# Four q buffers, three v buffers, a gate product over two blocks and one key per operation in a fused attention and gated FFN kernel

## The chip, the core and the metric

The kernel runs on one core of one Trainium2 chip. The metric is the device time of one execution in microseconds (us); lower is better. Engine names follow the profile: PE is TensorE (PEld its weight loads), DVE is VectorE, ACT is ScalarE, POOL is GpSimd and SP is SyncE. POOL issues the loads from HBM, SP the output stores and the DMA transposes.

## What is computed

Pooled attention feeds a feed-forward layer with a convolved gate. Cut to what matters:

```
B, H, S, D = 8, 8, 576, 64           # q, k, v: (B, H, S, D) float32
k_p, v_p = means over 8 neighbouring positions of k and v       # 72 of 576 rows stay
attn = softmax(q @ k_p^T / 8)
x = (attn @ v_p) with the heads side by side                    # (B, 576, 512)
h = max(x @ w_in, 0)                                            # (B, 576, 1024)
conv = sum over 3 taps of conv_w[tap] * h shifted by tap - 1    # along the sequence
out = (h * sigmoid(conv)) @ w_out                               # (B, 576, 512) float32
```

## The kernel before

The eight batches go in four groups of two (g0 to g3). A group has nine attention tiles of 128 rows: tiles 0 to 3 belong to its first batch, tile 4 is shared, 5 to 8 belong to the second.

- **Loads and preparation.** A batch's q, k and v come in by POOL queue, cast to bf16 in tiles of 128 partitions. q is transposed on PE in two halves (`prep_q`, L578) into PSUM and copied to `qT` by DVE or ACT (`copy_q`, L588). k is pooled by matmuls for b0 and b1 (`prep_k`) and, from group 1 on, for a whole group on DVE in three halving additions (`pool_pair`, L520), turned on PE (`turn_pair`, L526) and copied to `kT` (L539). v is pooled on DVE in three additions (L548) and masked into `vm` (L552). Rings hold 2 buffers of q (`qp`), 2 of v and 1 of k (`kk`).
- **Attention of a tile.** Scores on PE (L630, or L617 in quarter form), the row maximum on DVE (`negm`, L643), its subtraction on PE (group 0, L663) or DVE (`sd`, L655), exp on ACT (`e`, L681), the transposition of `e` on PE with a copy (groups 0 and 1: L692, L706) or as a DMA from SP (groups 2 and 3: L701), the values on PE (L717), reciprocal and division on DVE (`x`, L730, L732), and the transposition of `x` into `xT`, again on PE with a copy or as a DMA (L741).
- **FFN of a batch.** First layer on PE (`ffn_in`, L762; for b0 by tiles, `ffn_in_tile`, L783), relu on ACT (L771, L793) into `hT`. The convolution is matmuls with diagonal matrices in quarters of the PE array (`ffn_conv`, L844), two 128-wide blocks of d_ff at a time. ACT takes tanh of half of it into `tg` (L855). `ffn_gate` adds 1 on DVE (L872 for even blocks, L867 twice for odd ones, where the halves are swapped) and multiplies by `hT` into `gT` (L873), once per block: 8 products a batch. The second layer (`ffn_out`, L878) takes 36 tiles of 8 matmuls; ACT or DVE copies each tile out (L889) and SP stores it (L901).

Each engine executes its instructions in the order of its program; an instruction that waits holds up those behind it. That order is made by the class `Graph`: each piece of work is an `Op` with a key, with estimates of time on each engine, and with the buffers (`Token`) that it uses. `Graph.order` places them one after another: whichever can start next and has the lowest key goes first, and a copy that DVE or ACT may do goes where it can start. In the kernel before, keys come from a few numbers per class (`ATT`, `OUT`, `PREP_V` and others, and `NUDGE` per class and batch). The estimates only set the order: on the chip, semaphores release the instructions.

The waits of POOL's queue matter too: at most eight loads are under way, and a load whose buffer is in use waits for it, with everything behind it.

Of the kernel before, what the change touches and what calls it, by code (L numbers as in the profile page):

```python
# [33 lines left out]
class Graph:  # L34
# [8 lines left out]
    STAY = 2454.96  # L43
    LAZY = 7.6
    BLOCK, PRELUDE, FETCH, FETCH_LOADING = 256, 66, 3.4, 6.2
    BEAT, PHASE, HALVE, RAISE = 3.413, 0.7, 0.56, 0.85
    BESIDE_LOADS = 3.5
    SPARES = 150
    IN_FLIGHT = 8
    ATT = -1061.14  # L50
    SPREAD = -6040.17
    PREP_K = -4446.75
    KPOOL = -172.25
    KTURN = 242.29
    PREP_Q = 12175.88
    PREP_V = 17420.36
    GATE = 249.38
    CONV = -19287.15
    QCONV = -11687.66
    OUT = 13057.35  # L60
    LAST = 18152.59
    FIRST = 19180.99
    V0 = -19763.16
    DW = 22027.64
# [4 lines left out]
    URGENT = -28942.38  # L69
    NUDGE = {  # L70
# [203 lines left out]
def kernel(  # L274
# [826 lines left out]
    def prepared(g, t):  # L1101
# [3 lines left out]
        return need  # L1105

    def add_att(g, t, key):
        key += nudge("a", groups[g][t >= 5])
        rows = rows_of(g, t)
        b0 = groups[g][0]  # L1110
        split = len(parts(g, t)) == 2
# [158 lines left out]
```

## Time and profile before

| what | before |
|---|---|
| median of 3 runs (lowest, highest) | 248.94 us (248.41, 249.13) |
| profiled execution, its own time | 248.62 us |
| its span, first to last instruction | 246.9 us |
| PE, DVE, ACT busy | 218.5, 175.9, 149.1 us |
| mean granted PE clock | 0.975 of full speed |
| loaded and stored by DMA | 31.51 MB |

Of the 248.62 us of the profiled execution, 246.9 lie between its first and last instruction and 1.72 around them; its own time is 0.32 below the median of the three runs. Busy times of PE and PEld overlap, and a matmul's row includes its latency: four matmuls of 512 columns that follow each other have rows of 0.38 each and take 0.86 together. How far PE is from its work is therefore read from the idle time between its rows.

### The profile page before, as it was taken

Reading aid. Unit: us, or ns where it says so; the run is one execution under the profiler, and the core shown is the slowest. Engines: PE = TensorE matmul, PEld = TensorE weight load, DVE = VectorE, ACT = ScalarE, POOL = GpSimd, SP = SyncE. Lnnn points to the kernel's source line nnn. Section 1 sums busy time; section 2 is a strip of 40 time slices with the busy share of each in tenths; the row PEclk is TensorE's granted clock in tenths of the full one; section 3 lists DMA queues with packets and bytes.
Section 4 is the critical chain, followed back from the end, with each engine's and each line's share of the span. In section 5 each row is a group of like instructions: output and inputs, shape, how many; then the busy total and the mean of one; then the engine's idle time right before and its main releaser. Section 6 shows DMA issues by size and latency. Waiting matters only on the chain.

```text
span 246.9 us, 7525 instructions
## 1 busy us (share of the span) xinstructions
PE 218.5 (89%) x3206; PEld 149.4 (61%) x3206; DVE 175.9 (71%) x397; ACT 149.1 (60%) x245; POOL 27.9 (11%) x45
## 2 busy tenths in 40 slices
PE   7187999899699999968999992999999899999992
PEld 2174898776566566746764651776764477676440
DVE  7278757999999989789999992466689701965200
ACT  2046568688797666658676731575784456766531
POOL 7931303010320012200000100000000000000000
PEclk9779999999999999999999998899999999999998
DMA  6999999990799749913744799388125965600475
GB/s 92 176 203 207 208 206 208 205 191 5 105 185 240 168 75 210 206 24 61 93 88 93 145 136 130 70 142 144 22 48 125 127 127 120 128 4 3 92 165 127
DMA packets 44006, 31.51 MB, mean 128 GB/s; under 512 B 23596, under 2 KB 39364, under 8 KB 43972
## 3 DMA queue, kind: packets, MB, share of 16 engines
q0 software_dynamic: 16288, 16.26, 41.4%
q1 hardware_dynamic: 27604, 14.64, 32.2%
q8 instruction: 25, 0.41, 0.7%
q14 instruction: 9, 0.07, 0.2%
q10 hardware_dynamic: 80, 0.13, 0.1%
HBM read 32.52 MB, written 9.44 MB: 170 GB/s over the span
## 4 chain that ended last, share of the span: by engine, by line
PE 39%; DVE 32%; DMA 16%; ACT 5%; issue 5%; POOL 2%; DVEq 0%; ACTq 0%; POOLq 0%
PE psum L878 11%; PE psum L762 11%; DVE gT L873 6%; DMA eT<-e 6%; DVE negm L643 5%; PE psum L844 5%; DVE gT L867 4%; DMA qp<-in_q_dram 4%; DMA v<-in_v_dram 4%; DVE sd L655 4%; DVE x L732 3%; PE psum L783 3%; PE psum L717 3%; DVE v L548 3%; ACT tg L855 2%
## 5 line engine op out<-in xcount | busy, mean ns | idle before, releaser
L878 PE MATMUL psum<-w_out_sb,gT 128*128 128x512 bf16 x288 | 69.6, 379 | 0.3 <-ACT tg L855 0.2
L762 PE MATMUL psum<-xT,w_in_sb 128*128 128x288 bf16 x448 | 62.8, 290 | 0.7 <-ACT tg L855 0.6
L762 PEld LDWEIGHTS <-w_in_sb 128*128 128x128 bf16 x448 | 42.1, 99 | 14.5 <-issue 0.8
L771 ACT ACTIVATE hT<-psum 128x576 bf16<-128x576 f32 x56 | 35.3, 650 | 23.8 <-PE psum L762 23.6
L855 ACT ACTIVATE tg<-psum 128x576 bf16<-128x576 f32 x64 | 37.9, 649 | 12.3 <-PE psum L844 8.9
L878 PEld LDWEIGHTS <-gT 128*128 128x128 bf16 x288 | 26.1, 98 | 24.9 <-issue 0.4
L844 PE MATMUL psum<-hT,dw 64*64 64x288 bf16 (+4 forms) x1152 | 30.2, 246 | 0.0
L844 PEld LDWEIGHTS <-dw 64*64 64x64 bf16 x1152 | 24.3, 107 | 9.7 <-issue 9.1
L889 ACT COPY osb<-psum 128x512 f32<-128x512 f32 (+1 forms) x34 | 19.7, 580 | 16.6 <-PE psum L878 14.2
L643 DVE TENSOR_REDUCE negm<-psum 128x8 f32<-128x576 f32 (+1 forms) x36 | 26.4, 749 | 2.5 <-PE psum L630 1.9
L732 DVE TENSOR_TENSOR x<-psum,r 128x512 bf16<-128x512 f32 x36 | 24.9, 691 | 1.2
L681 ACT ACTIVATE e<-sd 128x576 bf16<-128x576 f32 x27 | 18.2, 682 | 10.0 <-DVE sd L655 9.2
L717 PE MATMUL psum<-vm,eT 128*128 128x130 bf16 (+5 forms) x240 | 18.4, 224 | 6.3 <-DMA eT<-e 5.5
L730 DVE RECIPROCAL r<-psum 128x8 f32<-128x8 f32 x36 | 7.2, 201 | 22.1 <-PE psum L717 22.0
L717 PEld LDWEIGHTS <-eT 128*128 128x128 bf16 (+1 forms) x240 | 14.5, 101 | 11.6 <-DMA eT<-e 6.6
L867 DVE TENSOR_SCALAR gT<-tg 64x576 bf16<-64x576 bf16 x64 | 20.0, 313 | 1.2
L655 DVE TENSOR_TENSOR sd<-psum,negm 128x576 f32<-128x576 f32 x27 | 19.8, 749 | 0.3
L872 DVE TENSOR_SCALAR tg<-tg 128x576 bf16<-128x576 bf16 x32 | 9.8, 306 | 10.8 <-ACT tg L855 10.8
L630 PE MATMUL psum<-kT,qT 128*128 128x144 bf16 (+1 forms) x136 | 12.8, 226 | 3.8 <-DVE kT L539 1.3
L873 DVE TENSOR_TENSOR gT<-tg,hT 128x576 bf16<-128x576 bf16 x32 | 14.7, 458 | 1.1
L873 DVE TENSOR_TENSOR gT<-gT,hT 128x576 bf16<-128x576 bf16 x32 | 14.6, 458 | 1.1
L630 PEld LDWEIGHTS <-qT 128*128 128x128 bf16 (+1 forms) x136 | 9.3, 98 | 7.8 <-issue 5.1
(74 smaller groups left out, 206.5 us busy)
## 6 DMA issues: line engine op xcount, KB each, us to landing
out_dram<-osb SPq DMA_DIRECT2D x71, 128.0 KB, 2.4
v<-in_v_dram POOLq DMA_DIRECT2D x8, 512.0 KB, 12.0
qp<-in_q_dram POOLq DMA_DIRECT2D x7, 576.0 KB, 12.5
kk<-in_k_dram POOLq DMA_DIRECT2D x3, 1152.0 KB, 10.9
w_in_sb<-in_moe_w_in_dram POOLq DMA_DIRECT2D x2, 512.0 KB, 12.7
w_out_sb<-in_moe_w_out_dram POOLq DMA_DIRECT2D x1, 1024.0 KB, 18.7
kk<-in_k_dram POOLq DMA_DIRECT2D x2, 288.0 KB, 7.2
kk<-in_k_dram POOLq DMA_DIRECT2D x1, 576.0 KB, 14.2
```

The costliest lines, as they stand in the source:

```text
L630: nc.tensor.matmul(out=heads[lo:hi, f], lhsT=buf("qT", b)[:, f, a, t % 5 * P:t % 5 * P + hi - lo], rhs=buf("kT", b)[:, 2 * f + a, :], star ...
L643: nc.vector.tensor_reduce(out=a["m"][0:rows], in_=a["s"][0:rows, :, 0:2 * KW].rearrange("p a (h s) -> p a h s", s=Sp), axis=AX.X, op=OP.ma ...
L655: nc.vector.tensor_tensor(out=a["d"][0:rows], in0=a["s"][0:rows, :, 0:2 * KW].rearrange("p a (h s) -> p a h s", s=Sp), in1=a["m"][0:rows]. ...
L717: nc.tensor.matmul(out=a["o"][lo:hi, h // 4, (h % 4) * (D + 1):(h % 4 + x1 - x0) * (D + 1)], lhsT=a["eT"][:, j, lo:hi], rhs=buf("vm", b)[: ...
L732: nc.vector.tensor_tensor(out=a["x"][0:rows].rearrange("p (a h d) -> p a h d", a=2, d=D), in0=ov[:, :, :, 0:D], in1=r[0:rows].unsqueeze(3) ...
L762: nc.tensor.matmul(out=banks(ps)[:, j, 0:SC], lhsT=w_in_block(dc, fb), rhs=buf("xT", g)[:, dc, i * S + j * SC:i * S + (j + 1) * SC], start ...
L771: nc.scalar.activation(out=buf("hT", b)[:, fb, :].rearrange("p (a s) -> p a s", a=2), in_=banks(ps)[:, :, 0:SC], func=ACT.Relu, scale=0.5,)
L844: nc.tensor.matmul(out=banks(pss[r ^ c])[c * D:(c + 1) * D, j, lo:hi], lhsT=dw[r * D:(r + 1) * D, tap * n_fb + fb, :], rhs=hT[r * D:(r + 1 ...
L855: nc.scalar.activation(out=tg.rearrange("p (a s) -> p a s", a=2), in_=banks(ps)[:, :, 0:SC], func=ACT.Tanh, scale=0.5,)
L867: nc.vector.tensor_scalar(out=gate[r * D:(r + 1) * D], in0=tg[(1 - r) * D:(2 - r) * D], scalar1=1.0, scalar2=None, op0=OP.add)
L873: nc.vector.tensor_tensor(out=gate, in0=tg, in1=buf("hT", b)[:, fb, :], op=OP.mult)
L878: nc.tensor.matmul(out=bank(ps)[0:rows, :], lhsT=buf("gT", g)[:, fb, t * P:t * P + rows], rhs=w_out_sb[:, fb, :], start=(fb == 0), stop=(f ...
```

## The change

Four edits. The rings of q and v get 4 and 3 buffers (from 2 and 2). The gate adds 1 for an even block into `gT` in place of `tg`, and one product over two blocks, 128 x 2 x 576, takes the place of two over 128 x 576. Every operation gets a key of its own from a table `KEYS`, in the order in which the operations were added, which overrides the class keys; some of the planner's estimates are changed as well. The rest of the diff gives the operations further names for nudges.

```diff
     PIPE = {"PE": 0.24, "DVE": 0.14, "ACT": 0.14, "POOL": 0.10, "SP": 0.0}
...
-    STAY = 2454.96
-    LAZY = 7.6
+    STAY = 0.1228
+    LAZY = 0.4188
...
-    BESIDE_LOADS = 3.5
+    BESIDE_LOADS, HOLD = 4.5, 0.3
...
+    GAP = 0.0
+    KEYS = (
+        -1000.0, 2.454, -4.193, 1.702, -1000.0, -1000.0, 2.8993, 1.9366, 7.1326, -1.4149, 7.4, 7.98,
...
+    )
...
     def order(self):
+        for o, key in zip(self.ops, self.KEYS):
+            o.key = key
...
-                if any(e2 == e and key2 < self.URGENT and key2 < o.key and s2 < s + d - 0.1 for s2, e2, _, key2 in later):
+                if any(e2 == e and key2 + self.GAP < o.key and s2 < s + d - 0.1 for s2, e2, _, key2 in later):
...
                     o.end = s + d + fixed + (self.BESIDE_LOADS if s < wire else 0.0)
+                    free[e] += self.HOLD if s < wire else 0.0
...
-             "hT": 2, "gT": 2, "xT": 2, "qT": 3, "kk": 1, "qp": 2, "v": 2, "vm": 5, "kT": 5, "sd": 3, "r": 3, "s": 2}
+             "hT": 2, "gT": 2, "xT": 2, "qT": 3, "kk": 1, "qp": 4, "v": 3, "vm": 5, "kT": 5, "sd": 3, "r": 3, "s": 2}
...
     def ffn_gate(b, fb):
         g, i = where[b]
-        tg, gate = buf("tg", b, fb), buf("gT", g)[:, fb, i * S:(i + 1) * S]
-        if fb % 2:
-            for r in range(2):
-                nc.vector.tensor_scalar(
-                    out=gate[r * D:(r + 1) * D], in0=tg[(1 - r) * D:(2 - r) * D], scalar1=1.0, scalar2=None, op0=OP.add
-                )
-            tg = gate
-        else:
-            nc.vector.tensor_scalar(out=tg, in0=tg, scalar1=1.0, scalar2=None, op0=OP.add)
-        nc.vector.tensor_tensor(out=gate, in0=tg, in1=buf("hT", b)[:, fb, :], op=OP.mult)
+        tg, gate = buf("tg", b, fb), buf("gT", g)[:, :, i * S:(i + 1) * S]
+        if fb % 2 == 0:
+            nc.vector.tensor_scalar(out=gate[:, fb], in0=tg, scalar1=1.0, scalar2=None, op0=OP.add)
+            return
+        for r in range(2):
+            nc.vector.tensor_scalar(
+                out=gate[r * D:(r + 1) * D, fb], in0=tg[(1 - r) * D:(2 - r) * D], scalar1=1.0, scalar2=None, op0=OP.add
+            )
+        both = slice(fb - 1, fb + 1)
+        nc.vector.tensor_tensor(out=gate[:, both], in0=gate[:, both], in1=buf("hT", b)[:, both], op=OP.mult)
```

The table of keys is shown by what it moves. In the rows below an instruction has its line, its operation, output<-input and the output's shape; L478 to L514 of the changed kernel are L365 to L401 of the kernel before, and all other lines are 113 or 114 higher.

**POOL, the start of the program, before.** Ahead of these rows stand the first half of b0's k, 320 of 576 columns of its q, and b1's q (`qp_78`). The loads are bf16 in SBUF, so that 128x4x512 is 0.52 MB; `pm` is the pooling matrix and `ident` the identity for transpositions.

```order
L393 DMA w_in_sb_71<-in_moe_w_in_dram 128x4x512
L365 DMA qp_77<-in_q_dram 128x4x256
L365 DMA kk_79<-in_k_dram 128x2x576
L383 DMA v_88<-in_v_dram 128x4x512
L386 DMA v_88<-in_v_dram 64x512
L365 DMA kk_79<-in_k_dram 128x4x576
L393 DMA w_in_sb_70<-in_moe_w_in_dram 128x4x512
L413 AFFINE_SELECT pm<-pm 64x9x72 x2
masks.py:197 MEMSET ident 128x128
masks.py:199 AFFINE_SELECT ident<-ident 128x128
```

The same place now. Ahead stand only the first half of b0's k, 256 columns of its q and the second half of its k:

```order
L526 AFFINE_SELECT pm<-pm 64x9x72 x2
L496 DMA v_90<-in_v_dram 128x4x512
L499 DMA v_90<-in_v_dram 64x512
L478 DMA qp_77<-in_q_dram 128x4x320
masks.py:197 MEMSET ident 128x128
masks.py:199 AFFINE_SELECT ident<-ident 128x128
L478 DMA qp_78<-in_q_dram 128x4x576
L478 DMA kk_81<-in_k_dram 128x4x576
L478 DMA qp_79<-in_q_dram 128x4x576
L506 DMA w_in_sb_71<-in_moe_w_in_dram 128x4x512
L506 DMA w_in_sb_70<-in_moe_w_in_dram 128x4x512
```

The pooling matrix, the identity and all of b0 moved ahead of everything else, and both halves of `w_in` moved behind q of b1 and b2 and k of b1. Further on, all eight loads of q are issued before b4's v, and six of the eight loads of v before the last load of k.

**ACT, ahead of the first scores of group 1, before:** tanh and relu of b0 and b1, then the copies of `kT` and `qT` for group 1, and its first exp (`e`).

```order
L855 ACTIVATE tg_118<-psum 128x576
L855 ACTIVATE tg_119<-psum 128x576
L771 ACTIVATE hT_117<-psum 128x576
L539 CAST kT_85<-psum 64x4x72 x2
L539 CAST kT_86<-psum 64x4x72
L588 COPY qT_80<-psum 128x2x576
L588 COPY qT_81<-psum 128x2x576 x2
L681 ACTIVATE e_101<-sd_130 128x576
```

The same place now; the rows ahead of these are the first five tanh of b0, and no relu of b1 stands among them:

```order
L968 ACTIVATE tg_121<-psum 128x576
L968 ACTIVATE tg_123<-psum 128x576
L968 ACTIVATE tg_122<-psum 128x576
L701 COPY qT_82<-psum 128x2x576 x2
L701 COPY qT_83<-psum 128x2x576 x2
L652 CAST kT_87<-psum 64x4x72 x2
L870 COPY xT_117<-psum 128x4x128
L652 CAST kT_88<-psum 64x4x72 x2
L794 ACTIVATE e_104<-sd_133 128x576
```

Attention of group 1 moved ahead of the first layer of b1, and four copies of `qT` stand directly ahead of the `kT` that the first scores need; ACT now makes all four `kT` copies here, where DVE had one.

Over the whole program the matmuls are the same, except that one more tile's scores are in quarter form, and PE changes between the full, half and quarter array 81 times in both. The copies that DVE or ACT may do went to ACT more often: of `kT` in 64x4x72 DVE has 1 (6 before), of `qT` in 128x2x576 2 (5), of `xT` 3 (6), of `eT` 5 (4), of `osb` in 128x512 1 (2). SP has the same 107 DMAs besides its first; of the 18 transpositions of `e`, 9 now stand directly behind an output store (6 before).

## Rows read from the trace of the kernel before

**Rows 1.** Page, part 1: busy us (share of the span) and instructions of each engine
```profile
PE 218.5 (89%) x3206; PEld 149.4 (61%) x3206; DVE 175.9 (71%) x397; ACT 149.1 (60%) x245; POOL 27.9 (11%) x45
```

**Rows 2.** Stretches of the span: length, busy time (instructions) of each engine, granted PE clock, DMA share, GB/s
```profile
28.33:47.07 18.74, 17.70 (x323) 16.03 (x316) 13.43 (x28) 12.76 (x19) 3.11 (x4) 1.00 1.23 207
...
57.50:92.40 34.90, 32.30 (x467) 21.22 (x465) 33.53 (x69) 26.54 (x46) 4.87 (x6) 1.00 0.74 136
92.40:108.70 16.30, 14.13 (x192) 10.42 (x192) 13.50 (x28) 9.99 (x18) 2.70 (x4) 1.00 0.97 168
108.70:147.80 39.10, 36.76 (x574) 24.01 (x574) 37.48 (x81) 26.32 (x43) 0.76 (x1) 1.00 0.65 97
147.80:157.00 9.20, 4.83 (x34) 3.38 (x33) 2.23 (x4) 2.18 (x5) 0.00 (x0) 0.81 0.70 103
157.00:239.60 82.60, 80.89 (x1131) 52.71 (x1129) 46.33 (x112) 50.74 (x85) 0.00 (x0) 1.00 0.51 95
```

**Rows 3.** The same view, from the span's start
```profile
0.00:14.10 14.10, 7.51 (x50) 4.01 (x52) 7.46 (x33) 2.48 (x4) 11.28 (x23) 0.82 0.97 142
0.00:24.00 24.00, 15.09 (x163) 9.42 (x164) 15.45 (x46) 8.05 (x14) 13.91 (x26) 0.86 1.08 168
```

**Rows 4.** Timeline: start us, us, engine, line, instruction [idle before <- releaser]; the start
```profile
11.71 1.28 PE L578 MATMUL psum<-ident,qp 128*64 128x128 bf16 x20 [5.30 <-POOL ident masks.py:199]
...
15.03 2.04 PE L578 MATMUL psum<-ident,qp 128*64 128x128 bf16 x52
```

**Rows 5.** Timeline of PE, 137.7 to 140.9 us: how far instructions start apart
```profile
137.70 0.41 PE L630 MATMUL psum<-kT,qT 128*128 128x144 bf16 x4
137.95 1.03 PE L878 MATMUL psum<-w_out_sb,gT 128*128 128x512 bf16 x4
...
139.70 1.20 PE L578 MATMUL psum<-ident,qp 128*64 128x128 bf16 x36 [0.24 <-ACT osb L889]
```

**Rows 6.** Timeline of PE: the first convolution, two pairs of blocks
```profile
47.07 1.69 PE L844 MATMUL psum<-hT,dw 64*64 64x288 bf16 x64
```

**Rows 7.** Timeline, 60 to 66 us: ahead of the first scores of group 1
```profile
60.30 1.19 ACT L855 ACTIVATE tg<-psum 128x576 bf16<-128x576 f32 x2 [0.33 <-DVE gT L867]
61.21 0.47 PE L526 MATMUL psum<-pick,kk 128*64 128x64 bf16 x18 [0.46 <-DVE kk L520]
61.90 1.20 ACT L539 CAST kT<-psum 64x288 bf16<-64x288 f32 x3
63.01 2.13 ACT L588 COPY qT<-psum 128x1152 bf16<-128x1152 bf16 x2
64.48 0.41 PE L630 MATMUL psum<-kT,qT 128*128 128x144 bf16 x4 [1.29 <-DVE kT L539]
65.27 0.41 PE L630 MATMUL psum<-kT,qT 128*128 128x144 bf16 x4 [0.38 <-DVE qT L588]
```

**Rows 8.** Groups by shape, DVE: line, shapes, count | busy us, mean ns of one | idle before
```profile
L873 DVE TENSOR_TENSOR gT<-tg,hT 128x576 bf16<-128x576 bf16 x32 | 14.7, 458 | 1.1
L548 DVE TENSOR_TENSOR v<-v 128x1280 bf16<-128x1280 bf16 x8 | 6.5, 816 | 1.2 <-DMA v<-in_v_dram 1.2
```

**Rows 9.** Timeline of PE: the longest waits behind 100 us, and matmuls after one
```profile
106.52 0.47 PE L526 MATMUL psum<-pick,kk 128*64 128x64 bf16 x18 [1.62 <-DVE kk L520]
...
152.86 0.83 PE L717 MATMUL psum<-vm,eT 128*128 128x130 bf16 x6 [4.38 <-DMA eT<-e]
153.51 3.27 PE L762 MATMUL psum<-xT,w_in_sb 128*128 128x288 bf16 x16
...
172.67 2.13 PE L762 MATMUL psum<-xT,w_in_sb 128*128 128x288 bf16 x16
```

**Rows 10.** Chain that ended last, in order of time: start us, us, what
```profile
95.73 9.45 DMA v<-in_v_dram
...
146.10 6.72 DMA eT<-e
```

**Rows 11.** Page, part 6: DMA issues, median us from issue to landing
```profile
eT<-e SPq DMA_TRANSPOSE x18, 2.6
```

More of the change, by code (lines that the diff above doesn't have):

```diff
@@ L42 @@
     LEAVE = {(64, 64): 0.13}
-    STAY = 2454.96
-    LAZY = 7.6
+    STAY = 0.1228
+    LAZY = 0.4188
     BLOCK, PRELUDE, FETCH, FETCH_LOADING = 256, 66, 3.4, 6.2
     BEAT, PHASE, HALVE, RAISE = 3.413, 0.7, 0.56, 0.85
-    BESIDE_LOADS = 3.5
+    BESIDE_LOADS, HOLD = 4.5, 0.3
     SPARES = 150
     IN_FLIGHT = 8
[L50 to L64, printed above, removed]
+    ATT = 90.28
+    SPREAD = -122.92
+    PREP_K = 135.88
+    KPOOL = -99.86
+    KTURN = 15.09
+    PREP_Q = 1123.0
+    PREP_V = 2242.18
+    GATE = 390.96
+    CONV = 199.25
+    QCONV = -794.87
+    OUT = 412.5
+    LAST = 1107.48
+    FIRST = 803.11
+    V0 = -1430.11
+    DW = -368.65
     X_DMA = 4
@@ L68 @@
     BANKS = 8
-    URGENT = -28942.38
-    NUDGE = {
[13 rows of a table removed]
+    URGENT = -3053.56
+    GAP = 0.0
+    KEYS = (
[81 rows of a table added]
+    )
+    NUDGE = {
[39 rows of a table added]
     }
@@ L1107, in add_att @@
     def add_att(g, t, key):
-        key += nudge("a", groups[g][t >= 5])
+        key += nudge("a", groups[g][t >= 5]) + nudge("t", 9 * g + t)
         rows = rows_of(g, t)
@@ L1177, in add_ffn @@
                 for j in range(2):
-                    o = add(pe(*[SC] * 4), w + 3 * fb, lambda fb=fb, j=j, big=big: ffn_in(b, fb, j, big),
+                    o = add(pe(*[SC] * 4), w + 3 * fb + nudge("i", 8 * b + fb), lambda fb=fb, j=j, big=big: ffn_in(b, fb, j, big),
                             after=need + [win[fb // 4], o], uses=[big, xtok[g], htok[b]], mode=FULL, count=8)
-                relu[fb] = [add(act(0.65), w + 3 * fb, lambda fb=fb, big=big: ffn_relu(b, fb, big), after=[o],
+                relu[fb] = [add(act(0.65), w + 3 * fb + nudge("i", 8 * b + fb), lambda fb=fb, big=big: ffn_relu(b, fb, big), after=[o],
                                 uses=[big, htok[b]])]
@@ L1184, in add_ffn @@
             cbs, tgs = [token("ps", n=2) for _ in fbs], [token("tg", b, fb) for fb in fbs]
-            conv = add({"PE": 0.66}, w + 6 * f2 + Graph.QCONV, lambda f2=f2, cbs=cbs: ffn_conv(b, f2, cbs),
+            conv = add({"PE": 0.75}, w + 6 * f2 + Graph.QCONV + nudge("c", 4 * b + f2), lambda f2=f2, cbs=cbs: ffn_conv(b, f2, cbs),
                        after=relu[fbs[0]] + relu[fbs[1]] + dwo, uses=cbs + tgs + [htok[b], gtok[g]], mode=QUARTER, count=64 + 12 * i)
@@ L1188, in add_ffn @@
                 o = add(act(0.65), w + 3 * fb + Graph.CONV, lambda fb=fb, cb=cb: ffn_tanh(b, fb, cb), after=[conv], uses=[tg, cb])
-                gdone.setdefault(b, []).append(
-                    add(dve(0.307, *[0.307] * (fb % 2), 0.458), w + 3 * fb + Graph.GATE, lambda fb=fb: ffn_gate(b, fb), after=[o],
-                        uses=[tg, htok[b], gtok[g]]))
+                gated = add(dve(*([0.307, 0.307, 0.752] if fb % 2 else [0.307])), w + 3 * fb + Graph.GATE, lambda fb=fb: ffn_gate(b, fb),
+                            after=[o] + gdone.get(b, [])[-1:] * (fb % 2), uses=[tg, htok[b], gtok[g]])
+                gdone.setdefault(b, []).append(gated)
     def add_out(b, w):
@@ L1199, in add_out @@
             key = w + 3 * rounds[n] - 1 + Graph.OUT + (Graph.LAST if b == B - 2 else 0) if b < B - 1 else w + n
+            key += nudge("ot", 9 * g + t)
             sm, osb = token("ps"), token("osb", g, t)
```

132 rows, old and new, of tables (KEYS, NUDGE) are left out of this document.

## The prediction

> **What bounds the kernel now.** I read the page's busy shares first. PE is busy 89% of the span, DVE 71% [rows 1]: PE is the nearest to a bound, but a gate that is lighter on DVE pays only where PE waits for DVE. So the second view is the stretches, where PE's idle time is a stretch's length less its busy time [rows 2]. The first layer of b0 begins at 28.33, its convolution at 47.07. From 57.5 on PE idles 2.60, 2.17, 2.34, 4.37 and 1.71 us in the five stretches. DVE is full from 57.5 to 147.8 (33.53 of 34.90, 37.48 of 39.10), and PE is nearly so beside it. In 147.8 to 157 neither is full: DVE works 2.23 of 9.20, PE 4.83. From 157 to 239.6 PE idles only 1.71 in 82.6, so nothing that lightens another engine can pay there.
>
> The third view, the timeline, says what the waits are. PE's first transposition of q starts at 11.71 after 5.30 idle, released by the identity that POOL makes [rows 4]. Ahead of group 1's first scores it waits 0.46, 1.29 and 0.38 [rows 7]. At 106.52 it waits 1.62 for DVE's pooled k, and the chain of waits has a v load of 9.45 us ahead of that [rows 9, 10]. At 152.86 it waits 4.38 for a transposed `e` by DMA, which took 6.72 [rows 9, 10], against a median of 2.6 [rows 11].
>
> The profiled execution took 248.62; the sum is made against that. It is 0.32 below the median of the runs, less than 0.3% of the time (0.75 us), about the least that a measurement of this kernel can tell from no change.
>
> **1. The start.** POOL makes the identity earlier and has all of b0 loaded first, so the transpositions and b0's attention start earlier; b0's first layer is then bounded by `w_in`, which now stands behind q and k of b1 and q of b2. Ahead of its end 4.59 MB are to be moved (two tensors of 0.59 for b0, v 0.59, three of 0.59 for b1 and b2, `w_in` 1.05). By 24.0 the loads have moved 24 x 168 GB/s = 4.03 MB [rows 3], then 207 GB/s [rows 2]: 26.7. From moved to used I add 0.9: by 14.1, 142 GB/s have moved 2.0 MB [rows 3], what stands ahead of q's second part and it, and that is used at 15.03 [rows 4]. So the first layer starts at 27.5 or so, 0.8 earlier than 28.33.
>
> Between it and the first convolution there is less to do, since that work now fits ahead: 20 score matmuls (five tiles at 0.25, from 137.70 to 137.95), 36 transpositions of q (1.20) [rows 5], and 30 small matmuls (transpositions of `e` and `x`, subtraction, values) at 1.20/36, 1.0. That is 3.4 of the 18.74 [rows 2]. The convolution starts at 27.5 + 18.74 − 3.4 = 42.8, not 47.07: **−4.3**. If the earlier attention does not fit ahead, only the 0.8 stays; if the 1.04 us that PE idles in this stretch [rows 2] goes too and `w_in` is used as it lands, it is −6.
>
> **2. Group 1's first scores.** These now stand directly behind b0's convolution, with no first layer of b1 as cover. PE has about 7 us ahead of them: four pairs of blocks at 0.85 (1.69 for two [rows 6]), two preparations of q (2.4 [rows 5]) and some 1.2 of turns and small matmuls, two of 0.47 among them [rows 7]. From 42.8 it is ready at 49.8. ACT is not: from about 43.7 it has eight tanh at 0.6, four copies of `qT` at 1.07 and two casts of `kT` at 0.40 [rows 7], 9.9 us, to 53.6. PE waits 3.8 to 4.0, where it waited 2.13 in three pieces [rows 7]: **+1.9**. Queued behind it on PE are the attention of g1 and then b1's first layer. The ends are −1 (ACT's copies come between the tanh while the convolution still runs) and +3.4 (the wait is long enough for the clock to fall, as below, at 1.45).
>
> **3. The v load.** With a third buffer and all q loads early, v and k of the later batches no longer wait for a buffer that attention frees; the wait of 1.62 at 106.52 [rows 9] goes: **−1.6**. Its ends are −1.6 and 0 (the DVE that pools it is full, so the wait may only change its name).
>
> **4. The gate, and copies to ACT.** The row of a product, 128 x 576, has the 32 even blocks at 458 ns [rows 8]; the 32 odd ones take their place in the same line. Another product on DVE, 128 x 1280 bf16, takes 816: 0.51 ns per further column, so 1152 columns take 458 + 576 x 0.51 = 750. Thus 32 x (2 x 458 − 750) = 5.3 us leave DVE. The additions stay; they only write elsewhere. Between no saving at all (1152 columns at twice 458) and the whole second product (14.7 us), I take 750 because the row of 1280 columns brackets it. Eight copies (five of `kT`, three of `qT`) leave DVE too and cost ACT 5 x 0.40 + 3 x 1.07 = 5.2 [rows 7]; ACT is at 61% of the span [rows 1] and has the room, except in step 2. The price of the joint product is delay: an even block's gate is complete only with the odd one's. PE takes them up in the second layer, behind all eight, so one block's wait of up to 0.75 us a batch is covered by other matmuls, except in the full stretches.
>
> What does it bring? Only what PE waits for DVE. In 57.5 to 147.8 PE idles 2.60 + 2.17 + 2.34 = 7.11 [rows 2]; less 2.13 (step 2) and 1.62 (step 3), 3.36 are left. Half of the products and half of the copies fall into this stretch, some 4 us off a DVE that works 84.5 of 90.3 there. By share of its remaining load that would take the idle time to about 3.2, by its slack (5.8 to 9.8) to about 2.0; I take 2.5: **−0.9**, with ends at −3.4 and +2 (attention of g1, pulled forward, puts more of DVE's chains into the same stretch).
>
> The Trainium skill ("Perfetto Trace Analysis", section "Optimizing Scalar/DVE Operations") states a fixed cost of about 60 ns for each DVE operation on SBUF while the engine is busy, with a profiled latency of twice that. By that page 32 operations fewer free an estimated 1.9 us of DVE, not 5.3, and by it the sum would be 242.1, with 0.6 less of step 4. No row of this case has an operation's fixed cost alone.
>
> **5. The transposed `e` at 152.86.** The DMA was slow beside loads: 6.72 against 2.6 [rows 10, 11], while 103 GB/s moved [rows 2]. With loads issued earlier the last should be done near 100, long before this place, so the transposition takes about 2.6 and the wait of 4.38 shrinks by 6.72 − 2.6 = 4.1 at most. But the next chain takes its place: exp, transposition, values, division, `x` transposed, first layer of b4. I leave 3.3 of waiting and the slow clock together, of 4.38 + 1.45 = 5.83: **−2.5**. The 1.45 is the clock: in this stretch it was granted at 0.81 [rows 2], that is partly at 1.2 instead of 2.4 GHz after the wait, and 16 matmuls of the first layer took 3.27 where they take 2.13 later [rows 9], 1.14, the other small ones some 0.3. Ends: −5.8 (nothing left) and +2 (a transposition queued behind a store waits as well as the new chain).
>
> **6. Edits at nothing, nearly.** One more tile has its scores in quarter form; the mode switches are 81 in both. I add **+0.3**. The stretch from 157 and the tail hold the same matmuls with 1.71 idle [rows 2]: 0.
>
> Sum: −4.3 + 1.9 − 1.6 − 0.9 − 2.5 + 0.3 = −7.1, so 248.62 − 7.1 = **241.5 us**.
>
> **Rivals.**
>
> *Only the front gain stays.* Steps 1 and 2 hold, but DVE is still full in the middle, so attention pulled forward brings back as much waiting as steps 3, 4 and half of 5 take. For it: DVE at 96% in both full stretches [rows 2], and one wait at 106.52 that names DVE, not a DMA [rows 9]. Then −4.3 + 1.9 − 1.2 + 0.3 = −3.3: 245.3. Chance 0.15.
>
> *Transpositions behind stores (slower).* SP's queue is in order. Nine of the 18 transpositions of `e` stand directly behind a store, six before; a store waits for its copy out of PSUM, and PE needs the `e` behind it. If two more of them are late as at 152.86, each costs 4.38 and 1.45 of clock: 241.5 + 2 x 5.83 = 253.2. It decides from the second such place on; with one, 247.3 would still be faster than before. Against it: of 18 only one was waited for that long [rows 9]. Chance 0.10.
>
> *Nothing happens at the start.* POOL's queue is in order and eight loads are under way at most, so four q buffers let nothing start that the wire could carry: it already carries 207 GB/s up to 47 [rows 2]. If `w_in`, further back now, comes later by what the attention gains, step 1 gives nothing, step 2 costs 1.9, and steps 3 to 5 give back about that: 248.5. Chance 0.07.
>
> *Better.* All waits of steps 2 to 5 go: 248.62 − 4.3 − 1.0 − 1.6 − 1.5 − 3.2 = 237. Chance 0.08.
>
> **How the numbers follow.** The forecast has 0.60. Its terms vary by about 2.5 us together, 239 to 244. To leave out no more than 2 in 10 the range takes in the rival that keeps the front gain and the better case, and stops short of the slower one: 237.0 to 247.0. Faster by over 0.3% (below 248.2): forecast, front gain and better, 0.83, less a little for a forecast whose ends add up badly, 0.82; within 0.3%: the rival of the start, 0.08 with that little; slower: 0.10.
>
> **What would show it.** Right: first transposition of q near 8 instead of 11.71; first convolution near 42.8; a wait of about 4 ahead of group 1's first scores, released by ACT's `qT` or `kT`; the product in the form 128 x 2 x 576 at about 750 ns, x32; no wait for pooled k of over 1 us; and no load under way behind 100, with the wait for `e` near 150 at most 3.3. Wrong: the convolution at 46 or later (step 1), a product at 900 (step 4), PE idle as long as before between the first convolution and 147 although DVE has less to do (steps 3 and 4), or several waits on transposed `e` with a store ahead in SP's queue.

## The result, and the profile after

The changed kernel took **237.18 us** (median of 4 runs, 237.03 to 238.33), against 248.68 (245.78 to 249.13) for the kernel before in the same comparison; the ratio is 0.9566 with a 95% interval of 0.9498 to 0.9634. That is 11.5 us less, where 7.1 were forecast: 0.2 us inside the lower edge of the range, in the direction that was forecast, with 1.6 times the gain. Times here are medians of all executions, while the ratios compare only those that ran in the fast one of two states; where the two differ, the ratio decides.

The profiled execution is the slowest of the four, 238.33, with a span of 236.6. Part 1 of its page, busy time by engine, answers to [rows 1]:

```profile
PE 219.2 (93%) x3222; PEld 151.5 (64%) x3222; DVE 166.8 (71%) x353; ACT 155.3 (66%) x258; POOL 27.9 (12%) x45
```

PE does the same work in a shorter span; DVE has 9.1 us less, ACT 6.2 more. The stretches, with columns as in [rows 2], cut where the program stands at about the same work:

```profile
8.02:29.88 21.86, 19.87 (x338) 14.49 (x337) 16.87 (x40) 13.20 (x23) 10.48 (x16) 0.86 1.24 206
29.88:42.46 12.58, 12.58 (x232) 11.95 (x230) 7.94 (x17) 8.99 (x12) 2.67 (x5) 1.00 1.23 208
...
42.46:55.56 13.10, 10.56 (x249) 7.74 (x247) 11.24 (x24) 11.90 (x20) 3.06 (x4) 0.99 1.23 207
55.56:90.00 34.44, 33.47 (x488) 24.04 (x489) 32.36 (x62) 27.04 (x48) 3.63 (x5) 0.95 1.05 184
90.00:138.00 48.00, 46.94 (x800) 32.41 (x797) 45.24 (x90) 36.69 (x62) 1.33 (x2) 1.00 0.49 85
138.00:157.00 19.00, 17.98 (x144) 12.07 (x144) 12.86 (x22) 9.79 (x17) 0.00 (x0) 1.00 0.63 129
157.00:229.00 72.00, 71.83 (x964) 46.53 (x963) 35.16 (x81) 44.65 (x76) 0.00 (x0) 1.00 0.49 96
```

The first convolution is at 42.46, not 47.07: 4.6 us of the span's 10.3 are gained ahead of it. Behind it PE idles 2.54, 0.97, 1.06, 1.02 and 0.17, together 5.8, where it idled 13.2 before from 57.5 to 239.6 [rows 2]. Of these 7.4 us, 5.7 arrive in the span. The rest is time in which PE is busy behind the convolution, some 1.5 us more than before: one attention tile moved there, three `blank` matmuls stand there and none did before (19 in all, 15 before, where the section on the change has the matmuls the same but for a tile's scores), and a spell of slow clock near 56 us stands where before there was one near 153. How they share it was not separated.

PE's timeline shows the start, and the place that the forecast feared:

```profile
8.02 0.64 PE L691 MATMUL psum<-ident,qp 128*64 128x128 bf16 x8 [3.26 <-POOL ident masks.py:199]
...
29.88 2.07 PE L896 MATMUL psum<-xT,w_in_sb 128*128 128x128 bf16 x32
...
42.46 1.11 PE L957 MATMUL psum<-hT,dw 64*64 64x288 bf16 x32
...
51.34 0.59 PE L594 MATMUL psum<-blank 128*128 128x512 bf16 x2 [0.33 <-ACT qT L701]
52.79 0.47 PE L639 MATMUL psum<-pick,kk 128*64 128x64 bf16 x18 [0.86 <-DVE kk L633]
...
54.21 0.66 PE L743 MATMUL psum<-kT,qT 128*128 128x144 bf16 x8 [0.17 <-ACT kT L652]
55.56 3.43 PE L991 MATMUL psum<-w_out_sb,gT 128*128 128x512 bf16 x8 [0.69 <-DVE gT L986]
```

The transposition starts at 8.02 and the first layer at 29.88, later than before (28.33); but then it takes 12.6 us to the convolution instead of 18.7. Ahead of group 1's scores PE waits 0.33, 0.86 and 0.17, and behind them 0.69. The `blank` matmuls between are work that nothing uses: the planner puts them where it expects PE to idle. The 8 matmuls at 55.56 take 3.43; the granted clock was at 0.50, that is 1.2 GHz, from 56 to 58.

The list of what PE waited for (line, releaser: us in total, times, longest), before:

```profile
PE psum L717 <- DMA eT<-e: 5.5, 3, 4.4
```

and after:

```profile
PE psum L691 <- POOL ident masks.py:199: 3.3, 1, 3.3
PE psum L830 <- DMA eT<-e: 1.8, 2, 1.0
```

The waits on a transposed `e` went from 5.5 to 1.8. The gate's row, to set against [rows 8]:

```profile
L986 DVE TENSOR_TENSOR gT<-gT,hT 128x1152 bf16<-128x1152 bf16 x32 | 24.3, 758 | 1.1
```

758 ns stand in place of 2 x 458: 5.06 us less by the rows, where 5.3 were worked out, or 158 ns per joint product. Rows of DVE can overlap, though, so that is not yet the time that the engine is freed. Where DVE's next instruction overlaps a product, it starts 0.37 us behind a single one, before,

```profile
74.90 0.46 DVE L873 TENSOR_TENSOR gT<-gT,hT 128x576 bf16<-128x576 bf16 x1
75.27 0.20 DVE L730 RECIPROCAL r<-psum 128x8 f32<-128x8 f32 x1
```

and 0.68 behind a joint one, after:

```profile
80.97 0.76 DVE L986 TENSOR_TENSOR gT<-gT,hT 128x1152 bf16<-128x1152 bf16 x1
81.65 0.75 DVE L768 TENSOR_TENSOR sd<-psum,negm 128x576 f32<-128x576 f32 x1
```

Back to back a joint product thus saves some 76 ns (2 x 376 − 676). The Trainium skill ("Perfetto Trace Analysis", section "Optimizing Scalar/DVE Operations") states about 60 ns of fixed cost for a DVE operation on SBUF while the engine is busy, and about twice that in a profile's latency; this trace has 76 and 158. About half of the products before are not overlapped, and DVE's busy time, with overlap counted once, fell by 4.8 us with the gate alone (175.9 to 171.1, b_gate below), 150 ns per joint product.

(Two counts in the section on the change were off by one: seven of the eight q loads, not all, are issued ahead of b4's v, and seven of the eight v loads, not six, ahead of the last load of k.)

### The profile page after: what moved, and what is told of

It reads as the page before. It is cut to its first block, busy times and chain, and to the rows that moved or that the text cites. A ratio compares the mean times of both kernels' runs of the same rounds, so it can differ in the third digit from the quotient of the medians.

```text
span 236.6 us, 7510 instructions
## 1 busy us (share of the span) xinstructions
PE 219.2 (93%) x3222; PEld 151.5 (64%) x3222; DVE 166.8 (71%) x353; ACT 155.3 (66%) x258; POOL 27.9 (12%) x45
## 4 chain that ended last, share of the span: by engine, by line
PE 74%; DVE 9%; ACT 5%; POOL 5%; DMA 3%; issue 2%; SPq 0%; POOLq 0%; ACTq 0%; DVEq 0%
PE psum L991 25%; PE psum L875 22%; PE psum L957 10%; PE psum L830 4%; PE psum L896 4%; PE psum L743 3%; DMA eT<-e 2%; DVE negm L756 2%; ACT tg L968 2%; PE psum L805 1%; PE psum L862 1%; POOL qp L478 1%; DVE gT L982 1%; PE psum L691 1%; DVE kk L633 1%
## 5 line engine op out<-in xcount | busy, mean ns | idle before, releaser
L991 PE MATMUL psum<-w_out_sb,gT 128*128 128x512 bf16 x288 | 71.6, 385 | 0.9 <-DVE gT L986 0.7
L991 PEld LDWEIGHTS <-gT 128*128 128x128 bf16 x288 | 26.7, 99 | 26.7 <-issue 1.7
L1002 ACT COPY osb<-psum 128x512 f32<-128x512 f32 (+1 forms) x35 | 20.2, 581 | 24.3 <-PE psum L991 21.4
L957 PE MATMUL psum<-hT,dw 64*64 64x224 bf16 (+4 forms) x1152 | 30.7, 246 | 0.7 <-DVE sd L768 0.5
L957 PEld LDWEIGHTS <-dw 64*64 64x64 bf16 x1152 | 24.9, 107 | 8.8 <-issue 7.5
L986 DVE TENSOR_TENSOR gT<-gT,hT 128x1152 bf16<-128x1152 bf16 x32 | 24.3, 758 | 1.1
L979 DVE TENSOR_SCALAR gT<-tg 128x576 bf16<-128x576 bf16 x32 | 9.8, 305 | 21.5 <-ACT tg L968 21.4
L701 ACT COPY qT<-psum 128x1152 bf16<-128x1152 bf16 (+2 forms) x15 | 15.0, 1036 | 1.6 <-PE psum L691 1.5
L661 DVE TENSOR_TENSOR v<-v 128x1280 bf16<-128x1280 bf16 (+2 forms) x24 | 13.0, 542 | 0.3
## 6 DMA issues: line engine op xcount, KB each, us to landing
v<-in_v_dram POOLq DMA_DIRECT2D x8, 512.0 KB, 13.2
```

The source lines that it names most:

```text
L957: nc.tensor.matmul(out=banks(pss[r ^ c])[c * D:(c + 1) * D, j, lo:hi], lhsT=dw[r * D:(r + 1) * D, tap * n_fb + fb, :], rhs=hT[r * D:(r + 1 ...
L986: nc.vector.tensor_tensor(out=gate[:, both], in0=gate[:, both], in1=buf("hT", b)[:, both], op=OP.mult)
L991: nc.tensor.matmul(out=bank(ps)[0:rows, :], lhsT=buf("gT", g)[:, fb, t * P:t * P + rows], rhs=w_out_sb[:, fb, :], start=(fb == 0), stop=(f ...
L1002: copy(out=osb[0:rows, columns], in_=bank(ps)[0:rows, columns])
```

## The experiments

To change one thing at a time, these kernels don't plan: the order that the planner gave (operation, engine, form, PSUM bank) is written into them as a list, and each engine takes its part of the list in that order. An operation enters the program once those it depends on are in it and its buffers are given free. Rings, gate or list are then changed alone. They ran in three sets, each beside the kernel before on the same chip: b_both, b_start, a_old_gate and a_old_loads (before: 247.47), a_again, ab_front, a_warm and a_fills (247.81), and a_best, ba_front, b_gate and a_q3 (248.70). The first two sets ran on one chip and the third on another, and by the executions behind the ratios the kernel before differs by 2.7 us between them; a smaller difference between times across the chips settles nothing. There the traces are used, cut at the first convolution.

| kernel | us (lowest, highest) | ratio to before (95%) |
|---|---|---|
| b_gate: before, new gate | 245.65 (244.56, 248.72) | 0.9864 (0.9812, 0.9916) |
| b_both: before, new gate and rings | 244.75 (242.71, 247.93) | 0.9923 (0.9869, 0.9977) |
| b_start: before, POOL's start reordered | 250.51 (249.32, 252.03) | 1.0172 (1.0071, 1.0273) |
| ba_front: old order to the first convolution, then new | 242.16 (241.43, 242.40) | 0.9734 (0.9692, 0.9775) |
| ab_front: new order to there, then old | 257.48 (256.88, 261.82) | 1.0475 (1.0393, 1.0556) |
| a_again: the changed kernel | 237.26 (236.74, 237.85) | 0.9652 (0.9586, 0.9719) |
| a_old_gate: changed, old gate | 240.11 (239.94, 240.77) | 0.9770 (0.9695, 0.9846) |
| a_q3: changed, 3 buffers of q | 240.40 (239.72, 241.29) | 0.9670 (0.9626, 0.9714) |
| a_old_loads: changed, old rings, loads by need | 263.61 (260.87, 266.05) | 1.0626 (1.0488, 1.0764) |
| a_warm: changed, blanks at the start | 238.42 (237.56, 240.00) | 0.9700 (0.9624, 0.9776) |
| a_fills: changed, blanks near 53 us | 236.72 (236.24, 236.90) | 0.9621 (0.9576, 0.9666) |
| a_best: a_fills, mask and maxima earlier | 236.02 (235.53, 236.61) | 0.9492 (0.9456, 0.9528) |

### The gate alone, and gate with rings

```diff
 # b_gate: the kernel before, its own order
-    ffn_gate: two products of 576 columns
+    ffn_gate: one product of 2 x 576 columns for two blocks
 # b_both: besides
-    "qp": 2, "v": 2
+    "qp": 4, "v": 3
```

Expected of b_gate: 

> The kernel before with the new gate alone: order and rings as before. DVE has 5.1 us less work. Theory A (of the 2.7 us of b_both the gate gives about 2, the rings the rest): 245 to 246.5 against 247.5 or so. Theory B (the rings gave it): within 0.7 us of the kernel before.

Expected of b_both: 

> The order of the kernel before, instruction for instruction, with the new gate and the rings of 4 and 3. Theory A (the order brings most of the gain; gate and buffers only help where the old order waited for DVE or for v): the first convolution stays at 47, the wait of 1.62 on pooled k goes, some 0.5 to 1 us of other waits on DVE too: 245.5 to 247.5 us. Theory B (gate and buffers carry the part of the gain behind the first convolution, 5.7 us): 242 to 244 us with the same start.

The gate alone gives 3.05 us by the medians (248.70 to 245.65) and 3.4 by the ratio, gate and rings together 2.7 (247.47 to 244.75) and 1.9: by the time of the whole kernel the rings add nothing that can be told. b_gate is where theory A had it; b_both lies between its two theories. The traces say more. From the first convolution to the end of the span (columns as in [rows 2]) the kernel before has

```profile
47.07:246.90 199.83, 181.85 (x2617) 120.88 (x2615) 143.12 (x316) 125.75 (x209) 9.60 (x13) 0.99 0.65 114
```

b_gate has

```profile
47.60:242.80 195.20, 179.89 (x2596) 120.99 (x2615) 138.32 (x284) 125.61 (x209) 9.60 (x13) 0.99 0.65 116
```

and b_both has

```profile
49.58:242.90 193.32, 180.53 (x2617) 120.19 (x2615) 138.23 (x284) 125.59 (x209) 8.23 (x11) 1.00 0.62 115
```

Each is one execution, but kernels with the same order behind the convolution repeat this length to some 0.3 us, on both chips: b_start, below, has 199.99 beside the 199.83 of the kernel before, and a_again, a_warm, a_fills and a_best have 192.3 to 192.6. So behind the convolution the gate gives 4.6 us, and the rings give 1.9 more in the old order; their 6.5 together is what theory B gave to them. The time of b_both doesn't show it because its first convolution comes at 49.58 in this execution, 2.5 us later than before. The granted clock was 0.50 there from 10 to 18 us; whether that made it late was not tested.

PE's timeline in b_gate shows where the gate's share comes from:

```profile
105.25 0.47 PE L596 MATMUL psum<-pick,kk 128*64 128x64 bf16 x18 [0.32 <-DVE kk L590]
...
149.59 0.83 PE L787 MATMUL psum<-vm,eT 128*128 128x130 bf16 x6 [3.03 <-DMA eT<-e]
```

The wait on pooled k fell from 1.62 to 0.32 and the one on transposed `e` from 4.38 to 3.03 [rows 9], with two buffers of v as before. So the wait that the forecast gave to the late v load goes, for 1.3 of its 1.6 us, with lighter work on DVE and no earlier load.

What the rings add is at the transposed `e`. In the kernel before, the last load of q waits 40.62 us for its buffer,

```profile
141.20 0.76 POOL L365 DMA_DIRECT2D qp<-in_q_dram  x1 [40.62 <-PE psum L578]
```

and the transposition that takes 6.72 from 146.10 on [rows 10] runs while that load lands. b_gate has the load at 139.26 and 5.34 for the transposition. In b_both the load goes out without a wait at 98.27, the transposition takes 2.62, and PE hardly waits at this place:

```profile
98.27 0.78 POOL L435 DMA_DIRECT2D qp<-in_q_dram  x1
...
152.03 0.53 PE L787 MATMUL psum<-vm,eT 128*128 128x130 bf16 x6 [0.17 <-DMA eT<-e]
```

PE's waits on a transposed `e` are 5.5 us in all before, 4.1 in b_gate, 2.1 in b_both and 1.8 in the changed kernel.

### The old gate in the new order

```diff
 # a_old_gate: the changed kernel, its own order and rings
-    ffn_gate: one product of 2 x 576 columns for two blocks
+    ffn_gate: two products of 576 columns
```

> The new kernel's order and rings with the old gate (two products of 576 columns, the even block's addition into its own buffer). Both theories: DVE has 5.1 us more work. Theory A (PE has little waiting on DVE left in this order): 0.3 to 1.5 us more, 237.5 to 239. Theory B (DVE is the limit of the middle, so half of the gate's work or more comes back as time): 2.5 us more or above, 240 or above.

240.11 against 237.18 and 237.26: 2.9 us more, theory B's side. Behind the first convolution a_again (the changed kernel, its order written out) has

```profile
42.66:235.20 192.54, 181.69 (x2649) 123.32 (x2647) 137.31 (x278) 131.60 (x223) 8.09 (x11) 1.00 0.67 123
```

and a_old_gate has 3.2 more:

```profile
42.46:238.20 195.74, 182.68 (x2649) 123.27 (x2647) 141.71 (x310) 131.87 (x223) 8.07 (x11) 1.00 0.66 121
```

The gate is worth about 3 us in the new order and 3 to 4.6 in the old one, more than half of the work that it takes off DVE.

### The front and the rest

The list of one kernel up to its first convolution, the other's from there. At that point both have done the same operations but a few (ahead of the old one are also one attention tile and two steps of pooling v).

```diff
 # ab_front
-    order: new
+    order: new up to the first convolution, then old
 # ba_front
-    order: new
+    order: old up to the first convolution, then new
```

> New gate and rings; the new order up to the first convolution (of the instructions ahead of it all but five are the same ones in both kernels), from there on the order of the kernel before. With b_both (old order throughout, 244.75) this tells what the front is worth. Theory A (front and rest add up): first convolution near 42.5, time 4 to 4.6 us below b_both, 240 to 241. Theory B (the old order behind it is bound by loads and DVE, so that an earlier front only waits longer): first convolution near 42.5, time 243 to 245, with the waits on pooled k or transposed e grown.

> New gate and rings; the order of the kernel before up to the first convolution (with its loads), from there on the new order. With b_both (old order throughout, 244.75) and the new kernel (237.2) it tells what the new order behind the convolution is worth alone. Theory A (it works on any front): convolution at 47, time 4.3 to 4.8 above the new kernel, 241.5 to 242. Theory B (front and rest belong together, as ab_front at 257.5 suggests: the loads that the rest counts on are issued in the front): waits of several us on loads or on what DVE makes of them behind the convolution, 245 or above.

ba_front comes close to theory A: 242.16. Beside b_gate, of the same set, that is 3.2 us by the ratios for rings and new order behind the convolution, without the new front. From its first convolution on it has

```profile
46.72:239.70 192.98, 177.58 (x2607) 122.13 (x2630) 134.21 (x273) 130.43 (x220) 6.73 (x9) 0.99 0.65 118
```

2.2 us less than b_gate, of which the rings give 1.9 in the old order already. So the new order behind the convolution is worth less than 1 us: 0.3 behind the old front (193.32 to 192.98), 0.8 with the new one (193.32 to 192.54). The new front is worth the 4.4 to 4.6 us by which the convolution comes earlier. ab_front is 10 us slower than the kernel before by the medians and 11.7 by the ratio, further off than theory B. In its profile, of the slowest of its executions (261.82), DVE and PE stand still together:

```profile
58.58 0.82 DVE L646 TENSOR_TENSOR v<-v 128x1280 bf16<-128x1280 bf16 x1 [15.18 <-DMA v<-in_v_dram]
...
60.30 0.61 PE L847 MATMUL psum<-ident,x 128*128 128x128 bf16 x4 [13.88 <-DVE x L830]
```

The old list has DVE pool b2's v here; the new front has POOL issue that load behind four q and a k. DVE takes its instructions in order, so the division that PE needs from 46 on stands behind that v, and PE goes on at 60. An order on one engine is right only for the loads that another engine's order brings; front and rest can't be credited apart in general, though one of the two crossings ran well.

### POOL's start alone

```diff
 # b_start: POOL's first pieces, the kernel before
-    k0, q0+, mask, q1, w_in1, q0, k0+, v0, k1, w_in0, pm, ident
+    k0, q0+, k0+, pm, v0, q0, ident, q1, k1, w_in0, w_in1, mask
```

> The kernel before with POOL's first twelve pieces in the new kernel's order (identity, pooling matrix and all of b0 ahead of b1 and w_in; q of b2 stays back, since there are two q buffers), nothing else. Theory A (PE's work from its first transposition on sets the first convolution, and the identity sets that): transposition near 8 instead of 11.7, convolution at 43 to 44 instead of 47.07, time 3 to 4 us less, about 245. Theory B (w_in, now behind b1's q and k, or the old order's waits take it back): convolution at 46 or later, time within 1 us of the kernel before.

Neither: 250.51, 3 us slower than before by the medians and 4 by the ratio, first convolution at 50.31. PE did start at 9.2, and then stood:

```profile
9.20 0.75 PE L648 MATMUL psum<-ident,qp 128*64 128x128 bf16 x20 [3.47 <-DMA qp<-in_q_dram]
...
13.59 1.29 PE L558 MATMUL psum<-pm,kk 128*64 128x144 bf16 x18 [3.48 <-DVE pm L499]
...
17.66 2.13 PE L648 MATMUL psum<-ident,qp 128*64 128x128 bf16 x36 [1.24 <-DMA qp<-in_q_dram]
```

and DVE's timeline shows why:

```profile
11.66 0.50 DVE L516 TENSOR_SCALAR vm<-mask 128x15 bf16<-128x15 bf16 x5 [6.33 <-POOL mask L504]
```

DVE's old order has the mask's columns ahead of the copy of `pm`; with the mask moved to the end of POOL's start, DVE waits 6.33 us for it and everything behind waits too. The identity alone does not make the early start: POOL's, DVE's and PE's orders changed together.

### What the buffers are for

```diff
 # a_q3
-    "qp": 4
+    "qp": 3
 # a_old_loads
-    "qp": 4, "v": 3
+    "qp": 2, "v": 2
-    POOL: q2 ahead of w_in; nearly all q ahead of v and k
+    POOL: loads of b2 to b7 by their first use
```

> The new kernel with three buffers of q in place of four, its order on every engine unchanged (with two, this order can't run at all: a load would wait for a buffer that is freed only behind it). Theory A (the third buffer of q is what the order needs, the fourth only spares POOL a wait): within 0.6 us of the new kernel. Theory B (with three, POOL's queue stands still behind a q load and the loads of k and v come late, as in a_old_loads): 2 us or more above, 239 or higher.

> The new kernel's order on PE, DVE, ACT and SP, with the old rings of 2 and 2 and the loads of b2 to b7 in the order of their first use, as far as two buffers let them go. Theory A (early loads matter: they take the transposed e out of the loads' way and spare the wait on v): loads end near 150, one or two waits on transposed e of 2 us or more, 240 to 243 us. Theory B (the order alone makes room for late loads): within 1 us of the new kernel, 236.5 to 238.5.

With three buffers of q the time is 240.40. The changed kernel ran beside other sets, so the traces are compared: behind the first convolution a_q3 has 4.0 us more than a_again.

```profile
43.04:239.60 196.56, 181.80 (x2624) 124.18 (x2647) 137.44 (x278) 131.67 (x223) 11.43 (x16) 0.99 0.65 121
```

PE's timeline has one new wait,

```profile
80.72 0.65 PE L860 MATMUL psum<-xT,w_in_sb 128*128 128x288 bf16 x4 [2.34 <-DVE sd L753]
```

and POOL's timeline has the cause, a q load that waits 21.52 us for its buffer, with three v and a k behind it in the queue:

```profile
51.90 0.74 POOL L463 DMA_DIRECT2D qp<-in_q_dram  x1 [21.52 <-PE psum L676]
...
56.54 1.03 POOL L470 DMA_DIRECT2D kk<-in_k_dram  x1
```

Theory B holds. With two and two the time is 263.61, further off than either theory had it:

```profile
36.89 1.17 PE L676 MATMUL psum<-ident,qp 128*64 128x128 bf16 x18 [11.49 <-DMA qp<-in_q_dram]
```

The transposition of b2's q, which the new order puts ahead of b0's first layer, waits 11.49 us for its load. So rings that are worth 1.9 us behind the convolution in the old order are what the new one stands on. The order of loads in a_old_loads is mine; a better one may exist, and its loss of some 25 us is not the buffers' price in general.

### The granted clock at two places

```diff
 # a_warm: 12 more blank matmuls ahead of the first transposition
+    PE 5.4 to 8.0 us: 12 x MATMUL psum<-blank 128x512
 # a_fills: 6 more, ahead of the turn of k and behind the first scores of group 1
+    PE 52 us: 3 x MATMUL psum<-blank 128x512
+    PE 55 us: 3 x MATMUL psum<-blank 128x512
```

> The new kernel, instruction for instruction (its order written out as a list), as the base for the three beside it: 236.8 to 238.5 us. Whether the granted clock falls near 56 us, as it did in the profiled execution (8 matmuls of the second layer in 3.43 us), is not the same in every execution: its other runs showed mean clocks of 0.99 and 1.0 with spans a microsecond shorter.

> The new kernel with 12 more of the matmuls on a blank tile that PE makes at the start, where it idles from 5.4 to 8.0 us. In the new kernel's profile the granted clock is 0.50 from 8 to 14 us, right behind that idle time. Theory A (the clock fell for want of work, and PE's own work bounds the start): clock at 1.00 from 8 on, first convolution 2 to 3 us earlier, 234 to 235.5. Theory B (DVE's maxima and q's loads bound those six microseconds): clock at 1.00, but the convolution at most 1 us earlier, 236.3 to 237.5. Theory C (the clock does not follow the work): no change.

> The new kernel with 6 more matmuls on a blank tile in the waits ahead of its second layer (three ahead of group 1's turn of k, three behind its first scores, where PE waited 0.86 and 0.69). Theory A (the low clock behind those waits costs 1.7 us where it happens): the 8 matmuls of the second layer take 1.73 in the profile, and the median falls by 0.5 to 1.7, to 235.5 to 236.7. Theory B (what PE gains there is waited for on DVE's product): within 0.5 us of the new kernel.

The clock differs between executions of one program. From 8 to 10 us the changed kernel's profile was granted half, its repetition all of it. First the one, then a_again (columns as in [rows 2]):

```profile
8.00:10.00 2.00, 1.98 (x20) 1.15 (x21) 1.69 (x7) 1.39 (x3) 2.00 (x3) 0.50 1.23 205
```

```profile
8.00:10.00 2.00, 1.98 (x20) 1.15 (x21) 1.70 (x7) 1.39 (x3) 2.00 (x3) 1.00 1.15 167
```

The first convolutions are at 42.46 and 42.66 us: the clock of the first microseconds cost nothing that shows, so PE's work there is not what sets the start. a_warm points the same way: at full clock PE is done early, waits 2.85 for the first maximum,

```profile
15.41 0.64 PE L763 MATMUL psum<-negm,ident 128*128 128x288 bf16 x2 [2.85 <-DVE negm L743]
```

and the clock falls there instead, to 0.50 from 16 to 18, where PE has the chain's work to do: its convolution starts at 43.48, 0.8 us later than in a_again. Its median is 238.42 (237.56 to 240.00, against 236.74 to 237.85), but the ranges overlap, so that it loses time is not shown. None of its three theories had the slow clock come later.

a_fills is at 236.72 (236.24 to 236.90) against a_again's 237.26 (236.74 to 237.85), 0.5 less, between its theories; the ranges overlap, so a gain is not shown. Its profile has the second layer at 55.57 with no wait, but in a_again's the clock had not fallen there either:

```profile
55.85 1.90 PE L976 MATMUL psum<-w_out_sb,gT 128*128 128x512 bf16 x8 [0.74 <-DVE gT L971]
```

That the blank matmuls hold the clock up is therefore not shown; a cost of theirs doesn't show either.

### The chain of the start, and a version that beats both

The chain that ended last, of the changed kernel (start us, us, what):

```profile
12.16 0.24 POOL mask L547
...
13.89 0.81 DVE v L661
14.69 1.33 DVE negm L756 x2
...
19.37 0.70 DVE x L845
...
20.12 0.40 PE psum L862 x4
```

POOL builds the head mask behind b1's loads and `w_in`; DVE spreads it (1.15, waiting 0.57), pools v, and only then takes the maxima on which PE waits. From 20.12 on the chain goes to and fro between PE and DVE's copies and maxima, up to 27.7, and is then mostly PE's.

```diff
 # a_best: a_fills, and
 POOL
-    ident, q1, k1, q2, w_in1, w_in0, mask, v1
+    ident, mask, q1, k1, q2, w_in1, w_in0, v1
 DVE
-    dw x2, kT, mask_wide, vm x5, v, negm x2, v x2
+    mask_wide, vm x5, kT, negm x2, v x3   (dw x2 behind the last negm of group 0)
```

> The new kernel with its head mask built by POOL ahead of b1's loads (8 instead of 12 us), DVE's two convolution matrices (1.83 us) moved from 9.2 us to behind the last maximum of group 0, the first two maxima ahead of the pooling of v, and the six more blank matmuls of a_fills. In the new kernel's chain the start runs through POOL's queue to the mask, then through DVE to the maxima (done at 16.0) and PE. Theory A (that chain sets the first convolution, not w_in): maxima done 1 to 1.8 us earlier, convolution at 41 to 41.8, time 0.5 to 1.8 below a_fills (236.72), 235 to 236.2. Theory B (w_in's landing, or PE's own work, sets it): convolution at 42.2 to 42.7, time as a_fills.

The timeline of DVE and PE in a_best:

```profile
12.76 1.42 DVE L742 TENSOR_REDUCE negm<-psum 128x8 bf16<-128x576 f32 x2 [1.41 <-PE psum L729]
```

```profile
28.89 2.08 PE L882 MATMUL psum<-xT,w_in_sb 128*128 128x128 bf16 x32
...
41.47 1.11 PE L943 MATMUL psum<-hT,dw 64*64 64x288 bf16 x32
```

The maxima are done 1.9 us earlier (14.18, not 16.03), the first layer starts 1.0 and the convolution 1.0 us earlier, and the time is 236.02 (235.53 to 236.61), below every execution of the changed kernel, at 0.9492 of the kernel before. The 0.7 us to a_fills (236.72) lie between chips, and the time alone doesn't tell them; the convolution does, at 41.47, in theory A's 41 to 41.8, where a_fills' profile has 42.46. Theory A holds: DVE's and POOL's order set the start in the changed kernel, not `w_in`. The moves were made together, so none is credited alone. In a_best the last half of `w_in` lands at 28.76, 0.1 us ahead of the first layer: moving the maxima further would meet it next.

## Why the prediction was right, and where its terms were not

- **The start (−4.3; measured −4.6).** Right in size by luck, and in part wrong in cause. The forecast had "b0's first layer is then bounded by `w_in`", at 27.5; it started at 29.88, though `w_in` had landed at 28.07, behind PE work that followed DVE's maxima, and a_best moved it by moving mask, convolution matrices and maxima. The other half was off by as much in the other direction: 12.6 us from there to the convolution, not 15.3. The 86 matmuls fewer were as counted (316 weight loads in [rows 2], 230 now), but PE's rows lost 5.1 us with them (17.70 to 12.58), not 3.4, and the 1.04 us of idle time, left to an end of the forecast, went as well. Two errors of 2.4 and 2.7 us cancelled.
- **Group 1's first scores (+1.9).** PE idled 2.54 from the first convolution to the second layer, against 2.13 before, and in the profiled execution the slow clock cost 3.43 − 1.90 = 1.5 more: +1.9. In a_again, with the clock up, about +0.7 (13.19 − 10.39 = 2.8 of idle time). So the agreement in size is luck: the forecast meant 3.8 to 4.0 of waiting, and had the slow clock only as an end. The place and the releaser of the first wait (ACT's `qT`) were as forecast; a single wait of 4 us did not come. Blank matmuls and a turn lie between its pieces, and the blanks cover about 1 us of it.
- **The v load (−1.6).** The wait went, but b_gate takes 1.3 of it away with the old rings. The step "no longer wait for a buffer that attention frees" named the wrong resource; the end given there, a DVE that is full, was the right one.
- **The gate (−0.9).** This is the term that was mis-sized: about −3 by the time and −4.6 behind the convolution in the old order, and 2.9 to 3.2 back when it is undone in the new. The product itself came as worked out (758 ns, 750 taken); the 5.3 us off DVE were added up from rows, and its busy time fell by 4.8. What failed is "only what PE waits for DVE", counted over the waits left when steps 2 and 3 had taken theirs: b_gate's own gains are at the pooled k, put down to step 3, and at the transposed `e`, put down to step 5, besides the waits counted here. That the `e` comes earlier because its exp stands behind DVE's shift is argued, not shown.
- **The transposed `e` (−2.5).** Waits 5.5 to 1.8, and no slow clock behind them (1.45 before): −5.1. The step itself is borne out by b_both, in the old order: with the last q load gone early the transposition took 2.62, no slow clock followed from 147 to 160, and 2.1 of the waits were left. The lighter gate alone has 1.35 of this. What was mis-sized is the chain that was to take the wait's place, 3.3 us of waiting and slow clock: the longest wait on a transposed `e` in b_both is 1.49.
- **Nothing from 157 on (0).** PE's idle time there fell from 1.71 to 0.17; a last stretch with slack was taken for one without.

Of the rivals, the one of transpositions behind stores did not occur: 9 stand behind a store and two waits of 1.0 at most are left. "Only the front gain stays" is answered by ba_front, where the gain behind the front came without the front. The one that the time met is "Better", 237 at a chance of 0.08: the terms were said to vary between 239 and 244, and that 237.18 lies in the range at all is luck, too. One of the signs failed narrowly, "no load under way behind 100": the last loads of v were issued at 98.42 and 99.18, and the DMA share was 1.02 from 100 to 110.

In sum, by the traces (spans of 246.9 and, in a_again, 235.2): 4.4 us from the front, 4.6 from the gate, 1.9 from the rings, and 0.8 from the new order behind the convolution. The forecast of 241.5 had the front right and everything behind it short by some 4, most of it the gate.

## What to carry to other kernels

Where an engine is full for a long stretch, count what its relief brings by the waits that any chain through it ends in, not by those that carry its name: some 5 us off DVE gave 3 to 4.6. Compare spans cut where the work is the same as well as whole times: a late start hid 1.9 us of the rings. Buffers and order are one thing: the rings gave 1.9 us in the old order, one buffer of q fewer cost the new one 4.0, and two and two with other loads some 25; a list of one engine put beside another engine's old list waited 14 us for a load that stands elsewhere in a queue. And follow the chain of the first 20 us to its source before filling the idle engine: here a mask of 0.7 us on POOL, moved by 3.7 us with two small moves on DVE, brought the convolution 1.0 us earlier, where a full clock at the start brought nothing.

## Not expected

- One program was granted 0.50 of the clock from 8 to 14 us in one execution and 1.00 in another, with the first convolution 0.2 us apart.
- Blank matmuls that keep PE busy early moved the slow clock to a later place (16 to 18 us), and the convolution came 0.8 us later.
- A DMA transposition's median from issue to landing is 2.6 us in both kernels; the 6.72 in the chain before [rows 10, 11] was one of 18. b_gate, with the old loads, shortens PE's wait on it to 3.03, though the transposition still takes 5.34 there; where the late q load is gone it takes 2.62.
